# Row sums turned in two 64-row pieces, six score banks in rotation, and a clear and four scatters moved

## The chip, the cores and the metric

The kernel runs on one core of one Trainium2 chip. The metric is the device time of one execution in microseconds (us). Five engines work side by side, each through its own instructions in order, and wait for each other by semaphores: TensorE (PE, matrix products and transposes), VectorE (DVE), ScalarE (ACT), GpSimd (POOL) and SyncE (SP, which issues most of the transfers).

## The reference

Three layers, all in float32:

```python
scores = q @ k.T / 8 + bias          # 2 batches, 8 heads, 768 rows, head size 64
scores = where(keep, scores, -1e9)   # keep: the 8 first columns and the last 96 before the row
a = exp(scores - max); a = a / (a.sum(-1) + 1e-9)
x = (a @ v)                          # 1536 x 512
h = x @ w_in; x = (h * sigmoid(h)) @ w_out          # 512 -> 2048 -> 512
e = argmax(x @ w_gate)               # one of 8 experts for each row
out = p[e] * sigmoid(x @ w_output_gate)[e] * (relu(x @ w1[e]) @ w2[e])
```

## The kernel before

The rows are cut in tiles of 128; a batch has six. Because of the band a tile of queries meets its own 128 keys and those of the tile before (whose place the global columns share). The **first batch** (tiles n = 0 to 5) is worked before everything else, in 24 **slots**: slot s = 4n + hp is the head pair hp of tile n. `slot_b(s)` writes the work of one slot as a pipeline over several head pairs:

- PE turns the exponentials of slot s-3 (`emit_tr`, L214: eight transposes of 64 rows, two row halves into two banks) and makes the scores of slot s+1 (`emit_qk`, L174) into other columns of the same two banks;
- DVE adds the bias table and finds the row minimum (`emit_tb`, L184, twice); ACT takes the exponential (`emit_exp`, L195, twice) and sums the row; ACT (DVE in the first eight slots) copies the turned tiles out (`emit_cp`, L220 or L221);
- PE multiplies the turned tile of slot s-4 with v (`emit_px`, L231) into the tile `px`, which is transposed: rows of it are head columns.

Once in four slots a tile is finished. DVE adds up and inverts the row sums (`emit_rs`), POOL spreads them over 512 columns (tile `rx`, L1043), PE turns `rx` (`emit_rb`, L238: four transposes of 128 rows into one bank, at the end of slot 4n+7), DVE copies the bank (L243) and multiplies `px` with it (L248), and POOL splits the product in a high and a low part (`put_xt`, L283 and L285). For n = 4 the turn stands at the end of slot 22, for n = 5 in slot 26, among the first steps of the next layer.

On the side the weights of the second layer, which come as 64-bit numbers, are decoded on DVE: `dec_op` puts nine single steps (L309, L310, L311 for three pieces of weight) into nine of the slots. Their scratch tile `dct` lies in a PSUM bank. POOL splits the decoded weights (L332, L339).

PSUM has eight banks. The score tiles (`xy`) and the turned sums (`rb`) rotate over five (`a`, `s20` to `s23`, by the counter `acnt`), `s1` and `pv` hold `px`, and `s1b` holds the warm-up products and then `dct`.

Slots 24 to 26 run beside the first steps of the second layer. Its loop has 5 x 16 steps: `s1_mm` (L361), `s1_ev`, `s1_sp`, `s2_mm` (L382 to L384, two steps behind), with chunk c = 0 being the tile pairs u = 0 and 1, and c = 1 to 4 one pair each. Beside chunks 1 to 3 the attention of the second batch runs (`slot`): there ACT's exponential is split in a high and a low half, the low half by POOL (`emit_l`, L202, for three of four head pairs), and both are transposed by a DMA (L205) before PE uses them (`emit_pv`, L260). Finished pairs pass the gates, one small part in each step from a queue `gq`: `gate1` (turn), `gate2` (logits), `gate3` (ranks, factor, and the first scatter of 128 rows to the DRAM table `xe`), `gate4` (the second scatter, L523, by POOL's own DMA). `rows_clear(0)` writes empty rows into the first window of `xe` from a zero tile, and later calls copy that window to the others.

The order on each engine is the order in which these functions are called; no scheduler moves anything.

Of the kernel before, what the change touches and what calls it, by code (L numbers as in the profile page):

```python
# [10 lines left out]
F32 = mybir.dt.float32  # L11
# [8 lines left out]
P = 128  # L20
# [3 lines left out]
def kernel(ctx, tc, qk, v, n_global, n_local, w_in, w_out, wg, w1, w2, out):  # L24
# [6 lines left out]
    SB=24  # L31
# [48 lines left out]
    wm=[]  # L80
    def warm(k):

        if not wm: wm.append(ps.tile([P,512],F32,tag="s1b",name="wm",bufs=1))
        for _ in range(k): T.matmul(wm[0].rearrange("p (a b) -> p a b",a=4),ones,ones[:,None,:].to_broadcast([P,4,P]),start=True,stop=True)
    def spread():

# [42 lines left out]
            if h%2 if dst.start<3 else h<2: (G if dst.start<3 else V).tensor_scalar(out=tabs[:,dst,h,:],in0=tabm['w'][0][:,3,src],scalar1=-8.0*2.0**-(h+1),scalar2=None,op0=ALU.mult)  # L129
            else: A.activation(out=tabs[:,dst,h,:],in_=tabm['w'][0][:,3,src],func=AF.Copy,scale=-8.0*2.0**-(h+1))  # L130

    atags=[['a','s20','s21','s22','s23']]; acnt=[0]; ded=[False]
    def abank(shape,name):
        tg=atags[0][acnt[0]%len(atags[0])] if not ded[0] else 'a'; acnt[0]+=1
        return ps.tile(shape,F32,tag=tg,name=name,bufs=1)
# [97 lines left out]
    rb={}  # L233
    def emit_rb(n):

        r=rs.pop(n)
        m=abank([P,KC,P],"rb")
        for k in range(KC): T.transpose(m[:,k,:],r[:,k*P:(k+1)*P],ident)  # L238
        rb[n]=m
        if n==SB//4-1: rb_copy(n,A)  # L240
    def rb_copy(n,e):
        m=rb[n]; x=rb[n]=attn.tile([P,KC,P],F32,tag="t",name="xn",bufs=3)
        if e is V: V.tensor_copy(x,m)  # L243
        else: A.activation(out=x,in_=m,func=AF.Copy)
    def emit_xx(n):
        if n<SB//4-1: rb_copy(n,V)
        x=rb.pop(n)
# [54 lines left out]
    def dct(tag):  # L302

        if tag not in pst: pst[tag]=ps.tile([P,512],I32,tag=tag,name="dct",bufs=1)
        return pst[tag]
# [18 lines left out]
    def dec_op():  # L324
        if not dops: return
        k,st=dops.pop(0)
        if st==0: wF[k]=mp.tile([P,512],I32,tag="wt",name="wt",bufs=2)
        r=wraw[k]; decode(wF[k],r[:,:,0],r[:,:,1],(st,),dct('s1b'))
        if st==2: del wraw[k]; wst[1,k%2]=k//2+1
    def spl_w(k,first=False):  # L330
        def cast(o,i):
# [87 lines left out]
    def rows_clear(e):  # L419
        win=lambda e: XE[e*CAP:e*CAP+WROWS,:].rearrange("(a p) d -> p a d",p=P)  # L420
        S.dma_start(win(e),win(0) if e else zr[0][:,None,:].to_broadcast([P,WROWS//P,XW]))
# [586 lines left out]
    def own(n): return 4*(n+2)>=SB  # L1008
    def slot_b(s):

        ev=[]
        n5,h5=divmod(s-LT-2,4); o5=0<=s-LT-2<SB
        n,hp=divmod(s,4); n1,h1=divmod(s-1,4); n3,h3=divmod(s-LT,4); n4,h4=divmod(s-LT-1,4)
        n2,h2=divmod(s-2,4); cur=s<SB; o1=0<=s-1<SB; o2=0<=s-2<SB; o3=0<=s-LT<SB; o4=0<=s-LT-1<SB
        def a_():
            if s<SB-3: want(min(s+WL,SB-1))
            elif cur: want(s+3)
            if s==0:
                m=two()
                for j in range(2): emit_qk(n,hp,j,m)  # L1020
            if cur: emit_tb(n,hp,0)
            if s+1<SB or o3: m=two()
            if o3: cp[0]=emit_tr(n3,h3,m)
            if s+1<SB:
                for j in range(2): emit_qk(*divmod(s+1,4),j,m)
            if s<3: warm(2)
            if s>=SB and o3: emit_cp(*cp[0],V)
            if o1 and s<SB: emit_exp(n1,h1)
            for d,h in TB.get(s-1,()):
                if d==0: tab_heads(slice(0,2),slice(0,2),(h,))  # L1030
        ev.append(a_)
        def a2():
            if cur: emit_tb(n,hp,1)
            if o3 and s<SB: emit_cp(*cp[0],A if DQ<=s<23 else V)
            if o1 and s>=SB: emit_exp(n1,h1)
            if o4: emit_px(n4,h4)
            if o3 and h3==3 and own(n3): emit_rb(n3)
            if o4 and h4==3 and not own(n4): emit_rb(n4)
            if o5 and h5==3 and not own(n5): emit_xx(n5)
            if o2 and h2==3:  # L1040
                for k in range(2): emit_rs(n2,k)
                r=attn.tile([P,512],F32,tag="t",name="rx",bufs=3)
                G.tensor_copy(r.rearrange("p (h d) -> p h d",h=H),rs[n2].to_broadcast([P,H,D])); rs[n2]=r  # L1043
        ev.append(a2)
        def b_():
            if cur: glob_k(n,hp)
            if h4==3 and o4 and own(n4): emit_xx(n4)
            if s==0: table(slice(0,3),(0,1))
            if s==1: table(slice(0,3),(2,))
            for d,h in TB.get(s,()):  # L1050
                if d: tab_heads(slice(2,3),slice(2,3),(h,))
            if hp==3 and 4*(n+1)<SB and cur: load_v(n+1)
        ev.append(b_)
        return ev
# [42 lines left out]
    with tc.manual_schedule():  # L1097
        params()
        want(7); load_v(0)
        table_ints()  # L1100
        warm(4)
        table_floats(slice(3,4),V)
        spread()
        warm(1)
        table(slice(3,4))
        table_floats(slice(0,3),A)
        tab_heads(slice(3,4),slice(3,4),range(H))
        rows_init()
        s=0
        while s<SB:  # L1110
            for k,e in enumerate(slot_b(s)):
                e()
                if k==0 and s in DQS: dec_op()
            if s==6: rows_clear(0)
            s+=1
            for x in WP.get(s,()): w_to(*x)
        atags[0]=['s20','s21','s22','s23']
        steps=[(c,f) for c in range(len(CH)) for f in range(FB)]
        pend=[]
        gq=[]  # L1120
        def run_ev(k):
            for _ in range(min(k,len(pend))): pend.pop(0)()
        def run_gates(k):
            for _ in range(min(k,len(gq))): gq.pop(0)()
        for g in range(len(steps)+LAG):
            live=g<len(steps)
            if live:
                c,f=steps[g]
                if g==4*FB: ded[0]=False
                if c==0:  # L1130
                    w_to(0,0,g+LI); w_to(0,1,g+(LO if g<LS else 1)); w_to(2,0,f+1)
                for u in CH[c]: s1_mm(u,f)
                for u in CH[c]: s1_ev(u,f)
                if c==0:
                    for _ in range(2 if g==0 else 1):
                        if s<SB+4: pend+=slot_b(s); s+=1
                    if g==3: atags[0]=['a']; gate_consts()
                    if g==8: gate_parts()
                    if f==FB-1: s=SB
                elif c<4 and s<NS+4 and (f>1 and f!=8 if c==1 else f%2==0):  # L1140
                    pend+=slot(s); s+=1
                run_ev((1,2,1,1,1)[c])
                for u in CH[c]: s1_sp(u,f)
                dec_rest()
                run_ev(5 if c==0 else 2 if c==1 else 3 if f%2 else 0)
                if g<=FB:
                    w_to(1,0,g+2); w_to(2,1,g-1); w_to(1,1,g)
                if g in (1,2,10,11,12,13,14): rows_clear(g if g<3 else g-7)
                if g==FB: load_v(SB//4)
            if g>=LAG:  # L1150
                c2,f2=steps[g-LAG]
                s2_mm(c2,f2)
                if live and g>=LAG+FB: run_gates(2 if g-(len(CH)-1)*FB in (2,4) else 1)
                if f2==FB-1:
                    first_=[lambda u=u: s2_ev(u) for u in CH[c2]]
                    if c2==0: first_.append(lambda: (atags.__setitem__(0,['a','s22','s23']),ded.__setitem__(0,True)))
                    gq[:0]=first_
                    at=len(gq)
                    for u in CH[c2]:
                        seq=[lambda n=n,fn=turn if u in PU else gate1: fn(n) for n in (2*u,2*u+1)]  # L1160
                        if u in PU: seq=[lambda u=u,fn=fn: fn(u) for fn in (piece1,piece2,piece3,piece4)]+seq+[lambda: None]*2
                        seq.append(lambda u=u: gate2(u))
                        if u==1: seq.append(lambda: None)
                        seq+=[lambda u=u,fn=fn: fn(u) for fn in (gate3,lambda u: gate4(u,1))]
                        for i,fn in enumerate(seq):
                            if at+i<len(gq): gq[at+i]=lambda fs=(gq[at+i],fn): [f() for f in fs]
                            else: gq.append(fn)
                        at=len(gq)-(4 if u in PU else 0)
                    run_gates(3 if c2==0 else 1)
                    if c2==len(CH)-2: gq.append(lambda: order(0))  # L1170
                    if c2==len(CH)-2: gq.append(moe2_open)
            if live and c>0:
                if f==0: load_wol(c,0); load_wol(c,1)
                if f+2<FB: load_wol(c,f+2)
            if g>=len(steps)-FB: moe2_pre(g-len(steps)+FB)
        moe2()
# [68 lines left out]
```

## Time and profile before

| | us |
|---|---|
| median of 3 runs (lowest to highest) | 560.42 (560.03 to 561.67) |
| the profiled execution's own time | 559.99 |
| its span, first to last instruction | 558.3 |
| PE busy | 546.5 (98%) |
| DVE busy | 379.7 (68%) |
| ACT busy | 310.2 (56%) |
| POOL busy | 168.0 (30%) |

The page cuts the span in 40 slices of 14 us. In the first three DVE, ACT and POOL are much busier than later (DVE 7, 9, 9 tenths; ACT 7, 9, 8; POOL 5, 7, 7), while PE shows 9 from the first to the last but one. A view by stretches gives busy microseconds of each engine; "x" is the number of instructions. In a timeline a row has start, duration, engine, line, operation and tiles, and in brackets how long its engine stood idle before it and what ended that. Rows may be merged, so a duration beside "x8" is that of all eight; where PE's rows overlap, the distance of starts is the cost.

### The profile page before, as it was taken

What the parts mean: (1) busy time and instruction counts of PE and PEld (TensorE: products, weight loads), DVE (VectorE), ACT (ScalarE), POOL (GpSimd) and SP (SyncE); (2) the same over time, 40 slices, a digit from 0 to 9 for tenths busy, and PEclk for the clock granted to TensorE, in tenths of its full rate; (3) what the DMA queues carried; (4) which work ended last, traced back from release to release, by engine and by line L of the source; (5) the groups of instructions that cost most, each with busy time, mean ns of one, the idle gap of its engine ahead of it and who ended that gap; (6) DMA issues with size and microseconds to landing.
All of it is one profiled execution on the core that took longest, in us unless ns stands there. A gap on an engine that the chain in (4) does not pass through costs nothing.

```text
span 558.3 us, 12046 instructions
## 1 busy us (share of the span) xinstructions
PE 546.5 (98%) x4048; PEld 467.7 (84%) x4048; DVE 379.7 (68%) x1114; ACT 310.2 (56%) x824; POOL 168.0 (30%) x231
## 2 busy tenths in 40 slices
PE   9999999999999999999999999999999999999993
PEld 4668999998888888888998989889887888888882
DVE  7997988883678737474634457548775976977950
ACT  7984444443654645445523436627755776867740
POOL 5775978673242430323001010210011010010011
PEclk9999999999999999999999999999999999999997
DMA  6763987995594877765593359129773967868500
GB/s 188 249 226 135 317 285 223 290 300 176 157 206 127 199 183 155 175 148 122 132 174 114 93 164 368 59 89 322 254 238 116 288 197 234 258 208 276 160 21 23
DMA packets 87531, 106.76 MB, mean 191 GB/s; under 512 B 35980, under 2 KB 50316, under 8 KB 87460
## 3 DMA queue, kind: packets, MB, share of 16 engines
q1 hardware_dynamic: 84980, 99.25, 60.7%
q0 software_dynamic: 2192, 6.39, 3.1%
q8 instruction: 34, 0.56, 0.4%
q14 instruction: 37, 0.30, 0.2%
q10 hardware_dynamic: 288, 0.26, 0.2%
HBM read 87.14 MB, written 17.66 MB: 188 GB/s over the span
## 4 chain that ended last, share of the span: by engine, by line
PE 81%; POOL 7%; issue 5%; DMA 3%; DVE 1%; ACT 1%; SPq 1%; POOLq 0%; ACTq 0%
PE s L361 20%; PE h L721 7%; PE s L382 6%; PE s L384 6%; PE s L383 6%; PE h L722 4%; PE y L754 4%; PE y L755 4%; PE y L756 4%; PE xy L174 3%; PE h L727 2%; PE pv L260 2%; POOL wol L345 2%; POOL g L371 2%; PE y L750 2%
## 5 line engine op out<-in xcount | busy, mean ns | idle before, releaser
L361 PE MATMUL s<-xT,wi 128*128 128x256 f32 x1152 | 152.5, 284 | 0.0
L361 PEld LDWEIGHTS s<-xT,wi 128*128 128x128 f32 x1152 | 147.2, 191 | 5.4 <-issue 0.3
L365 ACT ACTIVATE u<-s 128x256 f32<-128x256 f32 x96 | 36.4, 380 | 98.8 <-PE s L361 94.4
L382 PE MATMUL s<-woh,g 128*128 128x512 f32 x192 | 78.4, 408 | 0.0
L592 DVE TENSOR_TENSOR uq<-qr,uq 128x512 fp32r<-128x512 f32 x112 | 74.5, 689 | 3.3 <-ACT uq L591 1.4
L383 PE MATMUL s<-woh,g 128*128 128x512 f32 x192 | 75.6, 394 | 0.0
L367 DVE SCALAR_TENSOR_TENSOR s<-u,s 128x256 f32<-128x256 f32 x64 | 27.3, 426 | 60.1 <-ACT u L365 60.1
L591 ACT ACTIVATE uq<-qr 128x512 fp32r<-128x512 f32 x112 | 66.6, 625 | 1.4 <-DMA qr<-in_w_dram 1.4
L678 POOL DMA_INDIRECT out_dram<-y,ixt x17 | 19.0, 1120 | 154.3 <-ACT y L767 94.5
L195 ACT ACTIVATE t<-t,mx 128x256 f32<-128x256 f32 (+1 forms) x96 | 46.0, 485 | 0.4 <-DVE mx L184 0.3
L202 POOL TENSOR_TENSOR hl<-t,hl 128x512 f16<-128x512 f32 (+1 forms) x18 | 19.6, 1087 | 85.8 <-ACT g L370 37.4
L382 PEld LDWEIGHTS s<-woh,g 128*128 128x128 f32 x192 | 36.3, 189 | 6.9 <-issue 1.8
L383 PEld LDWEIGHTS s<-woh,g 128*128 128x128 f32 x192 | 36.3, 189 | 5.1
L384 PE MATMUL s<-wolr,g 128*128 128x512 f32 x128 | 39.8, 392 | 0.0
L371 DVE TENSOR_TENSOR g<-s,g 128x256 fp32r<-128x256 f32 x64 | 27.0, 422 | 16.3 <-ACT g L370 13.8
L734 DVE TENSOR_TENSOR h<-h,hs 128x192 f32<-128x192 f32 (+5 forms) x56 | 20.9, 373 | 25.3 <-ACT hs L733 25.2
L754 PE MATMUL y<-uq,hh 128*128 128x512 f32 (+1 forms) x88 | 36.7, 417 | 0.0
L370 ACT ACTIVATE g<-s 128x256 fp32r<-128x256 f32 x64 | 24.2, 378 | 21.4 <-DVE s L367 21.3
L755 PE MATMUL y<-uq,hh 128*128 128x512 f32 (+1 forms) x88 | 34.6, 394 | 0.0
L756 PE MATMUL y<-uq,hh 128*128 128x512 f32 (+1 forms) x88 | 34.6, 393 | 0.0
L736 ACT ACTIVATE hh<-h 128x192 fp32r<-128x192 f32 (+5 forms) x56 | 19.7, 352 | 24.9 <-DVE h L734 15.5
L721 PE MATMUL h<-xwT,uq 128*128 128x448 f32 (+5 forms) x144 | 32.5, 347 | 0.0
(283 smaller groups left out, 1097.8 us busy)
## 6 DMA issues: line engine op xcount, KB each, us to landing
qr<-in_w_dram SPq DMA_DIRECT2D x128, 256.0 KB
wolr<-wlo_d SPq DMA_DIRECT2D x64, 256.0 KB
wiraw<-in_w_in_dram SPq DMA_DIRECT2D x16, 512.0 KB
wraw<-in_w_out_dram SPq DMA_DIRECT2D x13, 512.0 KB
ring<-in_qk_dram SPq DMA_DIRECT2D x22, 256.0 KB
xe<-xe SPq DMA_DIRECT2D x7, 792.0 KB
wlo_d<-wol SPq DMA_DIRECT2D x16, 256.0 KB
xw<-xe SPq DMA_DIRECT2D x15, 264.0 KB
```

Of the source, the lines that this page charges most:

```text
L195: A.activation(out=t[:,j,:ce],in_=t[:,j,:ce],func=AF.Exp,scale=-1.0 if 4*n<SB else 0.125,bias=mx[n][:,h:h+1],accum_out=ss[n][:,h,0:1])
L361: T.matmul(t,w[:,ww,kc,:],x[:,xx,kc,:],start=(k==0),stop=(k==11)); k+=1
L371: (G if u_ in CH[0] else V).tensor_tensor(out=g[:,1],in0=t,in1=g[:,0],op=ALU.subtract)
L382: T.matmul(o,g[u][:,0,sl],wh,start=(f==0),stop=False)
L383: T.matmul(o,g[u][:,1,sl],wh,start=False,stop=False)
L384: else: T.matmul(o,g[u][:,0,sl],wl,start=False,stop=(f==FB-1))
L591: A.activation(out=t[:,0],in_=r,func=AF.Copy)
L592: (G if (i%2 if pool is None else pool) else V).tensor_tensor(out=t[:,1],in0=r,in1=t[:,0],op=ALU.subtract)
L721: for kc in range(KC): T.matmul(t[:,:2*W],uq[4*p+2*(f//4),kc][:,0,s],xwT[p,kc][:,:,:W],start=(kc==0),stop=False)
L754: T.matmul(o,hi,w[:,0],start=(f==0),stop=False)
L755: T.matmul(o,g[:,z:z+n],w[:,0],start=False,stop=False)
L756: T.matmul(o,hi,w[:,1],start=False,stop=(f==7))
```

## The change

- `emit_rb` takes two banks of the rotation by `two()` and turns the spread sums in eight transposes of 64 rows, as `emit_tr` does. It stands in the first part of a slot, behind `emit_tr` and ahead of the scores: for n = 0 to 4 in slot 4n+7 (n = 4 goes from slot 22 to 23), for n = 5 in slot 26. `rb_copy` copies two halves instead of one tile.
- `s1b` joins the rotation, which has six banks now, and the counter starts from 0 again after `spread`. The warm-up goes to `s1`. The nine decode steps lose their bank: they work in their result tile `wt`, in SBUF.
- `rows_clear(0)` is issued in slot 16 instead of slot 6.
- For the pairs u = 0 to 3 the second scatter stands one step later in the gate queue; so what follows it in the queue (the gates of u = 1 behind those of u = 0) also moves by a step.

```diff
-        if not wm: wm.append(ps.tile([P,512],F32,tag="s1b",name="wm",bufs=1))
+        if not wm: wm.append(ps.tile([P,512],F32,tag="s1",name="wm",bufs=1))
...
-    atags=[['a','s20','s21','s22','s23']]; acnt=[0]; ded=[False]
+    atags=[['s1b','a','s20','s21','s22','s23']]; acnt=[0]; ded=[False]
...
-        r=rs.pop(n)
-        m=abank([P,KC,P],"rb")
-        for k in range(KC): T.transpose(m[:,k,:],r[:,k*P:(k+1)*P],ident)
-        rb[n]=m
-        if n==SB//4-1: rb_copy(n,A)
+        x=rs.pop(n); m=rb[n]=two()
+        for k in range(KC):
+            for r in range(2):
+                o=slice(r*D,(r+1)*D)
+                T.transpose(m[r][:,k*D:(k+1)*D],x[o,k*P:(k+1)*P],ident[o,o])
     def rb_copy(n,e):
         m=rb[n]; x=rb[n]=attn.tile([P,KC,P],F32,tag="t",name="xn",bufs=3)
-        if e is V: V.tensor_copy(x,m)
-        else: A.activation(out=x,in_=m,func=AF.Copy)
+        for r in range(2):
+            o=x[:,:,r*D:(r+1)*D]; i=m[r][:,:KC*D].rearrange("p (k q) -> p k q",k=KC)
+            if e is V: V.tensor_copy(o,i)
+            else: A.activation(out=o,in_=i,func=AF.Copy)
...
-        r=wraw[k]; decode(wF[k],r[:,:,0],r[:,:,1],(st,),dct('s1b'))
+        r=wraw[k]; decode(wF[k],r[:,:,0],r[:,:,1],(st,))
...
             if o3: cp[0]=emit_tr(n3,h3,m)
+            if o4 and h4==3 and n4<SB//4-1: emit_rb(n4)
+            if o3 and h3==3 and n3==SB//4-1: emit_rb(n3)
             if s+1<SB:
                 for j in range(2): emit_qk(*divmod(s+1,4),j,m)
...
-            if o3 and h3==3 and own(n3): emit_rb(n3)
-            if o4 and h4==3 and not own(n4): emit_rb(n4)
+            if o3 and h3==3 and n3==SB//4-1: rb_copy(n3,A)
...
         spread()
+        acnt[0]=0
...
-            if s==6: rows_clear(0)
+            if s==16: rows_clear(0)
...
-                        seq+=[lambda u=u,fn=fn: fn(u) for fn in (gate3,lambda u: gate4(u,1))]
+                        seq+=[lambda u=u: gate3(u)]+[lambda: None]*(u<4)+[lambda u=u: gate4(u,1)]
```

PE, slots 10 to 13 of the kernel before (`xy` are the score banks, `t` exponentials, `ring` queries and keys, `rx` the spread sums of tile 1, `px` the products with v):

```order
L214 MATMUL xy<-ident,t 128x64 x8
L174 MATMUL xy<-ring_77 128x256 x2
L231 MATMUL px<-pT_383,vpr 64x128 x4
L214 MATMUL xy<-ident,t 128x64 x8
L174 MATMUL xy<-ring_76 128x256 x2
L231 MATMUL px<-pT_417,vpr 64x128 x4
L238 MATMUL rb<-ident,rx 128x128 x4
L214 MATMUL xy<-ident,t 128x64 x8
L174 MATMUL xy<-ring_76 128x256 x2
```

The same place of the changed kernel:

```order
L214 MATMUL xy<-ident,t 128x64 x8
L174 MATMUL xy<-ring_77 128x256 x2
L231 MATMUL px<-pT_388,vpr 64x128 x4
L214 MATMUL xy<-ident,t 128x64 x8
L240 MATMUL xy<-ident,rx 128x64 x8
L174 MATMUL xy<-ring_76 128x256 x2
L231 MATMUL px<-pT_421,vpr 64x128 x4
L214 MATMUL xy<-ident,t 128x64 x8
L174 MATMUL xy<-ring_76 128x256 x2
```

The turn of the sums moved ahead of the scores and the product of its slot, and four transposes became eight smaller ones.

POOL, the gates of pair u = 1 in the kernel before (`xr` gated rows, `gdi` their places, `hl` split exponentials, `vraw` and `vpr` values; the DMA rows are scatters):

```order
L517 COPY xr<-tok 128x2
L523 DMA xe<-xr,gdi 12288x528
L202 TENSOR_TENSOR hl<-t,hl 128x2x256
L154 TENSOR_TENSOR vpr<-vraw,vpr 128x512
L523 DMA xe<-xr,gdi 12288x528
L202 TENSOR_TENSOR hl<-t,hl 128x2x256 x2
L150 TENSOR_TENSOR vraw<-vraw,vpr 128x512
```

The same gates in the changed kernel:

```order
L202 TENSOR_TENSOR hl<-t,hl 128x2x256
L154 TENSOR_TENSOR vpr<-vraw,vpr 128x512
L519 COPY xr<-tok 128x2
L525 DMA xe<-xr,gdi 12288x528
L202 TENSOR_TENSOR hl<-t,hl 128x2x256
L525 DMA xe<-xr,gdi 12288x528
L202 TENSOR_TENSOR hl<-t,hl 128x2x256
L150 TENSOR_TENSOR vraw<-vraw,vpr 128x512
```

Both scatters moved behind the split of the values, and one split of exponentials stands on each side of the second.

SP, the transfers of slots 5 to 8 before (`ring` queries and keys, `xe<-zr` the clear, `wiraw` weights):

```order
L141 DMA ring_77<-in_qk_dram 128x2x256
L141 DMA ring_76<-in_qk_dram 128x2x256
L421 DMA xe<-zr 128x3x528
L144 DMA vpr<-in_v_dram 128x512
L295 DMA wiraw<-in_w_in_dram 128x4x256
L141 DMA ring_77<-in_qk_dram 128x2x256
```

Where the clear stands in the changed kernel:

```order
L144 DMA vpr<-in_v_dram 128x512
L141 DMA ring_77<-in_qk_dram 128x2x256
L423 DMA xe<-zr 128x3x528
L301 DMA woraw<-in_w_out_dram 128x1024
L144 DMA vpr<-in_v_dram 128x512
L297 DMA wiraw<-in_w_in_dram 128x4x256
```

The clear moved behind the last load of queries and keys for the first batch.

## Rows read from the trace of the kernel before

**Rows 1.** Stretch, its length, busy PE, PEld, DVE, ACT, POOL, clock, DMA share, GB/s:

```profile
14.50:25.60 11.10, 10.92 (x142) 7.25 (x140) 10.96 (x45) 10.42 (x42) 8.91 (x18) 1.00 0.90 282
25.60:41.00 15.40, 15.40 (x201) 10.20 (x197) 13.37 (x55) 14.42 (x57) 11.29 (x22) 1.00 0.64 212
...
60.00:140.00 80.00, 80.00 (x506) 72.64 (x506) 61.60 (x105) 35.90 (x84) 56.74 (x83) 1.00 0.80 262
```

**Rows 2.** Chain that ended last, slots 14 and 15: start, us, what:

```profile
26.84 0.49 PE xy L174 x4
27.33 0.59 PE px L231 x8
27.92 0.59 PE rb L238 x4
28.50 0.39 PE xy L214 x8
```

**Rows 3.** Timeline of slots 10 and 11, around the turn of tile 1:

```profile
19.42 0.61 POOL L1043 COPY rx<-rs 128x512 f32<-128x512 f32 x1
...
19.53 0.46 PE L214 MATMUL xy<-ident,t 64*128 64x64 f32 x8
...
19.71 0.42 DVE L184 CUSTOM_DVE_ANT_1 t<-xy,tabs 128x256 f32<-128x256 f32 x1
...
20.99 0.66 PE L238 MATMUL rb<-ident,rx 128*128 128x128 f32 x4
```

**Rows 4.** DVE by line and shape, first 46 us: count, then busy us, mean ns:

```profile
L243 DVE COPY xn<-rb 128x512 f32<-128x512 f32 x5 | 3.4, 684 | 0.0
L220 DVE COPY pT<-xy 128x256 f32<-128x256 f32 x7 | 2.6, 416 | 0.3 <-PE xy L214 0.3
...
L124 DVE TENSOR_SCALAR wk<-wk,pf 128x384 f32<-128x384 f32 x1 | 0.4, 414 | 0.0
...
L124 DVE TENSOR_SCALAR wk<-wk,pf 128x128 f32<-128x128 f32 x1 | 0.3, 287 | 0.0
```

**Rows 5.** Timeline, two places where DVE and POOL both work in SBUF:

```profile
179.86 1.16 POOL L150 TENSOR_TENSOR vraw<-vraw,vpr 128x512 f32<-128x512 f32 x1
...
180.02 1.02 DVE L506 CAST gdi<-gsm 128x2 uint32<-128x2 f32 x1
...
358.56 1.28 POOL L625 TENSOR_TENSOR ehl<-xr,ehl 128x512 fp32r<-128x512 f32 x1 [5.60 <-ACT ehl L624]
...
359.03 1.36 DVE L625 TENSOR_TENSOR ehl<-xr,ehl 128x512 fp32r<-128x512 f32 x1 [2.32 <-ACT ehl L624]
```

**Rows 6.** Timeline, two decode steps and the POOL operations beside them:

```profile
18.06 1.27 POOL L285 TENSOR_TENSOR xT<-xn,xT 128x512 fp32r<-128x512 f32 x1
...
19.11 0.69 DVE L310 SCALAR_TENSOR_TENSOR dct<-wiraw,dct 128x512 int32<-128x512 int32 x1
...
36.63 0.61 POOL L283 CAST xT<-xn 128x512 fp32r<-128x512 f32 x1 [0.49 <-DVE xn L248]
...
36.81 0.68 DVE L311 SCALAR_TENSOR_TENSOR wt<-wiraw,dct 128x512 int32<-128x512 int32 x1
```

**Rows 7.** Timeline, the clear's issue and the one load that PE waits for:

```profile
14.32 0.60 SPq L421 DMA_DIRECT2D xe<-zr  x1
...
23.69 0.30 PEld L174 LDWEIGHTS xy<-ring 64*128 64x128 f32 x4 [0.32 <-DMA ring<-in_qk_dram]
```

**Rows 8.** Timeline around the second scatter of pair u = 1:

```profile
187.86 0.99 POOL L523 DMA_INDIRECT xe<-xr,gdi  x1 [1.64 <-DMA xe<-xr,gdi]
188.87 1.18 POOL L202 TENSOR_TENSOR hl<-t,hl 128x512 f16<-128x512 f32 x1
...
195.01 0.76 PE L260 MATMUL pv<-vpr,pT 128*128 128x64 bf16 x20 [0.81 <-DMA pT<-hl]
```

**Rows 9.** Chain that ended last, the transfer between those two:

```profile
190.07 4.88 DMA pT<-hl
```

**Rows 10.** DVE's line L592 over the whole span: ns min/median/max, first and last start:

```profile
L592 DVE TENSOR_TENSOR uq<-qr,uq x112: 672/685/968, 339.5 to 529.5; 128x512 fp32r<-128x512 f32 x112
```

## The prediction

> **What bounds the kernel now.** I read the page's shares first: PE is busy for 98% of the span, so a gain must shorten PE's own work or one of its few waits. Then the view by stretches. From 60 to 140 us PE is busy for 80.00 of 80.00 us [rows 1]: a microsecond won before that point arrives at the end unless a transfer falls behind. Then the chain of waits in the first batch, because most of the change lies there. It runs from one PE group to the next, with nothing between: a slot is 0.49 (scores) + 0.59 (product with v) + 0.39 (turned exponentials) = 1.47 us, and a slot with a turn of sums has 0.59 more [rows 2]. By that chain PE alone bounds slots 12 to 23.
>
> The stretches warn against reading this alone. From 14.5 to 25.6 us DVE is busy for 10.96 of 11.10 us, more than PE's 10.92, with ACT at 10.42; from 25.6 to 41 PE has 15.40 of 15.40, ACT 14.42, DVE 13.37, POOL 11.29 [rows 1]. So up to slot 13 DVE is as much the bound as PE, and behind it a shorter PE has some 1.0 us (15.40 - 14.42) until ACT is the bound. Last I looked for PE's waits: 0.32 us at 23.69 for a load [rows 7] and 0.81 us at 195.01 for a transposing transfer [rows 8].
>
> **The change part by part.**
>
> *The turns.* Four transposes of 128 rows take 0.59 us; the eight of 64 rows have the shape of the turned exponentials, which take 0.39 [rows 2]. Six turns save 6 x 0.20 = 1.2 us of PE, five of them before 41 us and one in the full stretch behind. All of it is on PE's path, except where PE now waits in front of the turn. The turn moves up by a score group and a product, 0.49 + 0.59 = 1.08 us. What it needs has not moved: the spread sums from POOL, and its two banks. In slot 11 PE could begin it at 19.53 + 0.39 = 19.92. The spread sums end at 19.42 + 0.61 = 20.03, and one of the banks was last read by DVE's second score pass of slot 10, which ends at 19.71 + 0.42 = 20.13 [rows 3]. So PE waits 0.21 us there; before, the turn stood at 20.99 and waited for neither. Behind the waiting turn stand the scores of slot 12, for which ACT's copy and then DVE wait. I take 0.2 for slot 11 and another 0.2 for the turns of tiles 0, 2, 3 and 4 together: +0.4 (0 to +1.0, five such waits).
>
> *The copies.* One DVE copy of 512 columns, 0.684 us, becomes two of 256. Their rows show 0.416, but DVE starts the next before the last has ended, and 0.684 against 2 x 0.416 = 0.83 bounds the difference: 0 to +0.15 each [rows 4]. I take 0.
>
> *The decode steps.* Nine DVE instructions read and write SBUF only, where a PSUM bank served before. Alone they should cost the same: a two-input DVE instruction in SBUF with 512 columns has a median of 0.685 us [rows 10], the decode step 0.69 [rows 6]. But beside POOL it is different. At 359.03 the same kind of instruction took 1.36 us: POOL's own had begun at 358.56 and ended at 359.84, and DVE's was over 0.55 us behind that. A cast of two columns took 1.02 us from 180.02, until POOL's operation ended at 181.02 [rows 5]; the longest of the 112 two-input rows is 0.968 [rows 10]. So these six two-input steps will wait when POOL is in the middle of an operation. Laid on the trace of before: the step at 19.11 would wait until 18.06 + 1.27 = 19.33, 0.22 us, and the one at 36.81 until 36.63 + 0.61 = 37.24, 0.43 us [rows 6]. The other four start where POOL is between operations or about to start, and then POOL waits. I take +0.65, the sum of the two; from below 0, from above all nine steps at the mean of the two, 9 x 0.33 = +3.0. The first lies where DVE has 0.14 us of slack in 11.10 [rows 1]; the second has more room, but I count both in full.
>
> The Trainium skill says the same as a rule, and it speaks against this part of the change: in "SBUF — State Buffer", section "Who interferes with whom", a DVE instruction with two SBUF inputs and a POOL instruction that reads SBUF exclude each other, and the later one waits for the whole of the other. The rows at 359.03 agree (1.36 instead of 0.69 us). The other three steps have one input. "VectorE: DVE Perf Modes" of the Trainium skill, section "Mode 2×_2P", lets such an instruction run at twice the rate from SBUF to SBUF, holding the shared port meanwhile; L124 at 0.414 for 384 columns and 0.287 for 128 agrees for float32 [rows 4], and no run here shows it for this integer form with every second word read. By it the sum would have 3 x 0.2 us less on DVE, and three more waits.
>
> *The clear.* The clear's transfer goes out of slots 6 to 12 into those from slot 16 on, behind the last load of queries and keys that the first batch needs. The load that made PE wait 0.32 us at 23.69 [rows 7] comes earlier. DVE is full there, so I count 0; the gain is at most 0.32. The weights queued behind the clear in its new place are wanted only in the second layer, and the DMA share falls from 0.90 to 0.64 in that stretch [rows 1]: 0.
>
> *The scatters.* For pair u = 1 POOL stood 1.64 us before the second scatter, until the first had landed. The split of exponentials behind it began at 188.87, its transfer ran 4.88 us from 190.07, and PE waited 0.81 us [rows 8, 9]. Now the first scatter stands in front of that split and the second behind. The split can begin some 1.6 us earlier, of which the first scatter's 0.99 may take up to 0.99 back: between 0.65 and 1.64 earlier against a wait of 0.81. I take the whole wait as gone, -0.81 (0 from above). The gates of u = 1 move by one or two steps as a whole; PE has no other wait there to lengthen, and POOL is idle for most of those steps.
>
> *The sum*, against the profiled execution's 559.99: -1.2 + 0.4 + 0 + 0.65 + 0 - 0.81 = -0.96, so 559.03. That execution was 0.43 below the median of the runs, 560.42; as a median, 559.5. Its own range takes the ends of each term: all gains and no cost, -1.2 - 0.32 - 0.81 = -2.3 (558.1); the dearer DVE waits at half their bound and a scatter that gains nothing, -1.2 + 0.4 + 1.5 = +0.7 (561.1).
>
> **The rivals.**
>
> *DVE and POOL don't collide*, because in the new order the steps fall between POOL's operations. For it: POOL is idle for 2.2 of 11.1 us and 4.1 of 15.4 [rows 1]; against it the two pairs in rows 6. Then the DVE term is 0 and the load's wait counts: -1.2 + 0.4 - 0.32 - 0.81 = -1.93, 558.5.
>
> *The turns wait for POOL* (slower). A decode step holds POOL back for up to 0.69 us, and between two turns POOL has to do L283, L285 and the spreading in a row. Two such blocks move the end of the spread sums in slot 11 from 20.03 to 21.41, and PE stands from 19.92 until then, with the next scores behind it: 1.49 us. For the three turns with decode steps around them that is 4.5 us, less the 1.2 and 0.81: +2.5, 562.9. For it: the turn has lost its 1.08 us of lead, and POOL is busy for 80% of the first stretch. Against it: most steps start beside no POOL operation. It decides from 0.67 us for each of the three turns (2.0 / 3); below that the kernel is not slower.
>
> *The scatters' place changes nothing*: the 4.88 us of the transfer are themselves a queue behind other transfers, and PE waits as before. For it: the DMA engines are busy there. Against it: the transfer starts right behind the split. Then 560.3.
>
> **How the numbers follow.** Chances: my forecast 0.55 at 559.5, no collisions 0.20 at 558.5, turns waiting for POOL 0.12 at 562.9, scatters for nothing 0.13 at 560.3. A measurement of this kernel can tell about 0.3%, 1.7 us, from no change: faster means below 558.7, slower above 562.1. Faster: the 0.20, and a ninth of the forecast's share whose costs stay out, 0.06, together 0.26. Slower: 0.12. Within: 0.62. The range from 558.0 to 561.6 leaves out the slower rival for the most part and a little below.
>
> **What would show it.** In the changed trace: L240 at about 0.39 us for eight; the wait of PE before it and its releaser (DVE's L184 or POOL's `rx`); the decode rows L311 to L313 longer than 0.69 us where a POOL row ends within them; no wait for a load near 23.69; the first product of the second layer (L361 before) between 0.5 us earlier and 0.5 later than now; PE's wait at L260 near 195 gone. I am wrong if the decode rows stay at 0.69 while the stage still gains nothing, if PE stands for more than 0.67 us before the turns, or if a new wait appears in chunk 1.

## The result, and the profile after

| | before | after |
|---|---|---|
| median (lowest to highest), us | 560.38 (560.03 to 561.67), 6 runs | 566.01 (565.11 to 566.74), 6 runs |
| span of the profiled execution, us | 558.3 | 563.7 |
| PE busy, us | 546.5 | 546.3 |
| POOL busy, us | 168.0 | 170.9 |

The ratio is 1.0100, 95% interval 1.0087 to 1.0112: slower by 5.6 us, where 559.5 was forecast and 561.6 was the range's upper end. PE does no more work; it waits more. The view of waits sums PE's idle time by what ended it (total, times, longest):

```profile
PE xy L240 <- POOL rx L1046: 2.8, 3, 1.1
PE gl L473 <- DVE xT L287: 2.2, 1, 2.2
...
PE h L723 <- ACT eyo L677: 0.8, 1, 0.8
PE px L231 <- POOL vpr L163: 0.4, 1, 0.4
```

None of these four stood in the kernel before; its one large wait, for `pT` at 195.01 [rows 8], is gone. To see where the lateness arises I took the same matmul in both traces:

| place (start before, us) | later in the changed kernel by |
|---|---|
| scores ahead of the first turn (12.15) | -0.23 |
| product of slot 10, behind the first turn (18.94) | -0.39 |
| first product of slot 11 (20.40) | +1.15 |
| first batch over, L361 (41.96) | +1.89 |
| chunk 1 under way (154.37) | +1.50 |
| behind the logits of u = 1 (183.00) | +5.27 |
| behind the place of the old wait (199.88) | +4.48 |
| first h of the last stage (375.44) | +5.47 |
| near the end (530.53) | +5.35 |

The first -0.23 is the start of the program (between -0.2 and +1.0 in the profiled executions, also of kernels that are not changed there), the next -0.16 the first turn, for which PE did not wait. So there are three losses and one gain: first batch +2.1, gates +3.8, the last stage +1.0, and -0.8 for the old wait. The -0.4 ahead of chunk 1 is a wait for a load of weights (at 142.38 in the kernel before) that comes and goes between executions of all these kernels.

**The first batch.** The stretches answer [rows 1] (PE, PEld, DVE, ACT, POOL busy, clock, DMA share, GB/s); the second is longer here, since the batch ends later, and the last one is the place behind the logits:

```profile
14.50:25.60 11.10, 10.03 (x142) 6.71 (x144) 10.37 (x42) 10.01 (x40) 8.57 (x16) 1.00 0.61 184
25.60:42.80 17.20, 15.05 (x212) 9.77 (x210) 15.17 (x60) 14.88 (x58) 13.69 (x22) 1.00 0.72 247
60.00:140.00 80.00, 80.00 (x509) 72.78 (x508) 63.27 (x107) 34.85 (x80) 58.59 (x85) 1.00 0.83 268
178.20:181.70 3.50, 3.50 (x29) 3.28 (x26) 1.53 (x9) 0.21 (x1) 0.00 (x0) 0.51 0.58 137
```

Before, PE was idle for 0.18 us in the first and not at all in the second; now it is idle for 1.07 and 2.15 us, though no other engine is full either: they wait for each other in turn. The timeline answers [rows 3] and shows how:

```profile
19.14 0.46 PE L214 MATMUL xy<-ident,t 64*128 64x64 f32 x8
...
19.20 0.80 DVE L312 SCALAR_TENSOR_TENSOR wt<-wiraw,wt 128x512 int32<-128x512 int32 x1
...
19.40 0.67 POOL L159 COPY ring<-ring 128x32 f32<-128x32 f32 x1
...
20.01 0.61 POOL L1046 COPY rx<-rs 128x512 f32<-128x512 f32 x1
...
20.67 0.46 PE L240 MATMUL xy<-ident,rx 64*128 64x64 f32 x8 [1.07 <-POOL rx L1046]
...
20.97 0.65 PE L174 MATMUL xy<-ring 64*128 64x256 f32 x4
...
24.63 0.42 DVE L311 TENSOR_SCALAR wt<-wiraw 128x512 int32<-128x512 int32 x1
...
24.68 0.84 POOL L285 CAST xT<-xn 128x512 fp32r<-128x512 f32 x1
...
32.83 1.28 POOL L287 TENSOR_TENSOR xT<-xn,xT 128x512 fp32r<-128x512 f32 x1
...
33.15 1.23 DVE L311 TENSOR_SCALAR wt<-wiraw 128x512 int32<-128x512 int32 x1
...
34.04 0.41 POOL L159 COPY ring<-ring 128x32 f32<-128x32 f32 x1
...
34.39 0.61 POOL L1046 COPY rx<-rs 128x512 f32<-128x512 f32 x1
...
35.05 0.46 PE L240 MATMUL xy<-ident,rx 64*128 64x64 f32 x8 [1.09 <-POOL rx L1046]
```

POOL's copy of 32 columns (0.21 us otherwise) took 0.67 beside the decode step and ended just after it. `rx`, next on POOL, came 0.59 later than before, and PE stood from 19.60 to 20.67 with the scores of slot 12 behind the turn. At 33.15 the decode step was the late one (1.23), behind POOL's split of 32.83, and POOL's copy then waited for it in turn. The groups of the first 46 us (count, busy us, mean ns) show the collisions as a whole:

```profile
L312 DVE SCALAR_TENSOR_TENSOR wt<-wiraw,wt 128x512 int32<-128x512 int32 x3 | 2.6, 861 | 0.0
L311 DVE TENSOR_SCALAR wt<-wiraw 128x512 int32<-128x512 int32 x3 | 2.4, 786 | 0.0
L313 DVE SCALAR_TENSOR_TENSOR wt<-wiraw,wt 128x512 int32<-128x512 int32 x3 | 2.4, 786 | 0.0
...
L159 POOL COPY ring<-ring 128x32 f32<-128x32 f32 x16 | 4.8, 305 | 0.0
```

The decode steps cost 7.4 us instead of 6.2 (9 x 0.69 [rows 6]), and POOL's sixteen small copies alone 4.8 instead of 3.2.

**The gates of u = 1.** Timeline of PE and DVE:

```profile
173.54 0.63 PE L279 MATMUL ms<-ident,xa 128*128 128x128 f32 x4
...
174.94 0.62 PE L386 MATMUL s<-wolr,g 128*128 128x512 f32 x2
...
176.03 0.69 DVE L202 TENSOR_TENSOR hl<-t,hl 128x512 f16<-128x512 f32 x1
...
177.06 0.68 DVE L287 TENSOR_TENSOR xT<-ms,xT 128x512 fp32r<-128x512 f32 x1
177.80 0.86 PE L473 MATMUL gl<-wgb,gx 128*128 128x48 bf16 x24 [2.23 <-DVE xT L287]
...
178.49 2.91 PE L363 MATMUL s<-xT,wi 128*128 128x256 f32 x12
```

In chunk 1 one bank, `a`, serves the gates' tiles and the turned attention rows `ms` (`abank` while `ded` is set). Before, the logits `gl` took it first, then `ms`:

```profile
170.03 0.77 PE L471 MATMUL gl<-wgb,gx 128*128 128x48 bf16 x24
...
170.64 1.67 PE L361 MATMUL s<-xT,wi 128*128 128x256 f32 x12
...
172.75 0.64 PE L277 MATMUL ms<-ident,xa 128*128 128x128 f32 x4
```

The empty step of u = 0 moved the gates of u = 1 one step on, so `ms` takes the bank first, and `gl` waits until DVE, with its queue of that slot, has read it: 2.23 us. Behind this wait the granted clock fell to 0.51 over the stretch 178.2 to 181.7 (1.2 GHz); twelve L363 took 2.91 us, where twelve took 1.67 before.

**The last stage:**

```profile
375.60 4.49 PE L674 MATMUL ey<-uq,eg 128*128 128x512 f32 x18
...
380.17 0.69 ACT L677 ACTIVATE eyo<-ey,ex 128x512 f32<-128x512 f32 x1 [3.69 <-PE ey L674]
...
380.91 0.96 PE L723 MATMUL h<-xw,qb 128*128 128x384 f32 x4 [0.82 <-ACT eyo L677]
```

Here the rotation is `s1`, `s1b`, `a`, `pv`, and `ey` lies in `pv`. The counter stands at 99 where it stood at 94: the first `h` gets bank 99 mod 4 = 3, `pv`, instead of 2, `a`, and must wait until ACT has read `ey`. Before, it followed `ey` without a wait:

```profile
371.12 4.48 PE L672 MATMUL ey<-uq,eg 128*128 128x512 f32 x18
375.44 0.86 PE L721 MATMUL h<-xw,qb 128*128 128x384 f32 x4
```

### The profile page after: what moved, and what is told of

Its sections match the earlier page's. It is cut to its first block, busy times and chain, and to the rows that moved or that the text cites. A ratio compares the mean times of both kernels' runs of the same rounds, so it can differ in the third digit from the quotient of the medians.

```text
span 563.7 us, 12103 instructions
## 1 busy us (share of the span) xinstructions
PE 546.3 (97%) x4072; PEld 468.3 (83%) x4072; DVE 380.7 (68%) x1119; ACT 310.8 (55%) x825; POOL 170.9 (30%) x231
## 4 chain that ended last, share of the span: by engine, by line
PE 91%; POOL 3%; DVE 2%; issue 1%; DMA 1%; ACT 1%; SPq 0%; POOLq 0%; ACTq 0%; DVEq 0%
PE s L363 24%; PE s L384 8%; PE s L385 8%; PE s L386 8%; PE h L723 7%; PE h L724 4%; PE y L756 4%; PE y L758 4%; PE y L757 4%; PE xy L174 3%; PE pv L262 2%; PE h L729 2%; PE y L752 2%; PE y L751 2%; PE xm L713 1%; PE px L231 1%
## 5 line engine op out<-in xcount | busy, mean ns | idle before, releaser
L363 PE MATMUL s<-xT,wi 128*128 128x256 f32 x1152 | 153.7, 286 | 0.1
L363 PEld LDWEIGHTS s<-xT,wi 128*128 128x128 f32 x1152 | 148.4, 192 | 5.6 <-DVE xn L250 0.3
```

The costliest lines, as they stand in the source:

```text
L363: T.matmul(t,w[:,ww,kc,:],x[:,xx,kc,:],start=(k==0),stop=(k==11)); k+=1
```

## The experiments

Theory: three separate losses, the early turns together with the collisions, the gates' step, and the bank counter. Rivals: the late first batch makes the later waits; or the collisions alone are the loss.

**gates_before**, the changed kernel with

```diff
-seq+=[lambda u=u: gate3(u)]+[lambda: None]*(u<4)+[lambda u=u: gate4(u,1)]
+seq+=[lambda u=u,fn=fn: fn(u) for fn in (gate3,lambda u: gate4(u,1))]
```

> The changed kernel with the gate queue of before: no empty step ahead of the second scatters. Theory (the loss has three separate places: turns in the first batch +1.9, the gates of u = 1 +3.9, the first h +0.9): the logits of u = 1 (L473) stand again one step ahead of the turn ms, take bank a before it, and the wait of 2.23 us and the slow clock behind it (about 1.6 us) go, while the wait for pT near 195 comes back with 0.87: 566.0 - 3.9 + 0.9 = 563.0. Rival (the late first batch shifts the whole of chunk 1 and makes that wait; the gates' order has no part in it): the wait at L473 stays and the one for pT comes on top: 566.0 to 566.9.

562.68 (ratio to before 1.0033, 1.0021 to 1.0045). The wait at the logits and the slow clock are gone. But the wait for `pT` did not come back, which neither theory had.

**gates_u1**, the changed kernel with

```diff
-[lambda: None]*(u<4)
+[lambda: None]*(0<u<4)
```

> The changed kernel with the empty step for u = 1 to 3 only, not for u = 0: the gates of u = 1 stand where they stood before, and only the second scatter is a step later. Theory (the empty step of u = 0 pushes the logits of u = 1 behind ms; the spacing of u = 1's own scatters is what removes the wait for pT): the wait at L473 and the slow clock go, -3.9, and the wait near 195 does not come back: 566.0 - 3.9 = 562.1. Rival (the wait for pT went because the whole group moved): as gates_before, 562.7 to 563.0.

562.10 (1.0036, 1.0022 to 1.0050), as the theory said: the step of u = 0 costs 3.9 us by the medians, 3.6 by the ratios. PE's waits here are those of the first batch and the last stage alone.

**gates_alone**, the kernel before with the change's line for the gates.

> The kernel before with one edit: the empty step ahead of the second scatter for u = 0 to 3. Theory (the empty step of u = 0 alone puts the logits of u = 1 behind ms on bank a; nothing of the first batch is needed for it): PE waits about 2.2 us at the logits (L473 in the changed kernel), the wait near 195 goes: 560.4 + 2.2 + 0.6 - 0.9 = 562.3, and 563.7 if the clock falls as in the changed kernel. Rival (the late first batch made the wait): 560.4 - 0.9 = 559.5.

562.65 (1.0044, 1.0028 to 1.0060). The first batch is as before, and the same wait stands at the logits:

```profile
177.22 1.05 PE L471 MATMUL gl<-wgb,gx 128*128 128x48 bf16 x24 [2.23 <-DVE xT L285]
178.09 2.86 PE L361 MATMUL s<-xT,wi 128*128 128x256 f32 x12
```

So the late first batch has no part in it; that rival falls. That the bank makes the wait is read from the program, where `gl` reads nothing of `ms` or `xT`; no run gives `gl` a bank of its own. The clock fell in this execution too, but not in each: the six runs gave 563.27 to 564.30 where the mean granted clock was 0.991 or 0.992, and 561.34 to 562.03 where it was 0.995. By these two groups the fall costs about 1.8 us; by the traces, 1.5 (the gates cost 3.8 us with it and 2.3 in turns_behind_px without). The changed kernel's runs do not show it: five of six have 0.991 or 0.992, and the one with 0.996 took 565.96, no less than the others.

**h_bank**, the changed kernel with

```diff
-        atags[0]=['s1','s1b','a','pv']
+        atags[0]=['s1','s1b','a','pv']; acnt[0]+=3
```

> The changed kernel with three added to the bank counter where the last stage begins, so that its first h takes the bank it had before and not the one of ey. Theory (ACT's reading of ey holds the bank): PE's wait of 0.82 before the first h (L723) goes, 566.0 - 0.87 = 565.1, all else as it is. Rival (a transfer that lands late holds h, and the releaser named is only the last one seen): the wait stays, 566.0.

564.97 (1.0083, 1.0063 to 1.0103), 1.0 less than the changed kernel. `h` follows `ey` at once (before this it waited 0.82):

```profile
378.76 1.55 PE L674 MATMUL ey<-uq,eg 128*128 128x512 f32 x6
380.14 0.86 PE L723 MATMUL h<-xw,qb 128*128 128x384 f32 x4
```

**turns_behind_px**, the changed kernel with the two calls of `emit_rb` moved from the front of the slot to behind `emit_px`.

```diff
-            if o4 and h4==3 and n4<SB//4-1: emit_rb(n4)
-            if o3 and h3==3 and n3==SB//4-1: emit_rb(n3)
...
+            if o3 and h3==3 and own(n3): emit_rb(n3)
+            if o4 and h4==3 and not own(n4): emit_rb(n4)
```

> The changed kernel with the turns at their old place behind px (for n = 4 in slot 22), still 64 rows and two banks, decode steps still in SBUF. Theory (the waits come from the turn having lost 1.08 us of lead): PE's waits before L240 fall from 2.8 us in all to 0.5 or less, the first batch ends at most 0.4 later than before instead of 1.9: 566.0 - 1.6 = 564.4. Rival (POOL and DVE, which hold each other up, are late whatever the place): PE waits as long, for rx or for the copies of exponentials: 565.5 to 566.0.

563.66 (1.0059, 1.0041 to 1.0077), 2.35 less, more than the theory's 1.6. Its trace gives 1.6 for the first batch; the rest can be the clock, since one run in six had a mean granted clock below 0.994, where five of the changed kernel's had. No wait stands before L240. Left are the waits at the logits and at `h`, and two groups for POOL, behind operations of it that a decode step lengthened:

```profile
PE gl L473 <- DVE xT L287: 2.2, 1, 2.2
...
PE xy L174 <- POOL ring L159: 0.9, 2, 0.5
PE px L231 <- POOL vpr L163: 0.9, 1, 0.9
```

In this execution the wait of 2.23 us at the logits was not followed by a slower clock:

```profile
177.90 1.68 PE L363 MATMUL s<-xT,wi 128*128 128x256 f32 x12
```

**decode_sbuf**, the kernel before with

```diff
-decode(wF[k],r[:,:,0],r[:,:,1],(st,),dct('s1b'))
+decode(wF[k],r[:,:,0],r[:,:,1],(st,))
```

> The kernel before with one edit: the nine decode steps work in their result tile in SBUF and not in a PSUM bank. Theory (collisions lengthen DVE and POOL by 1 to 3 us, but the turns at the end of their slots cover it): decode steps with a mean of about 0.8 us instead of 0.69, the first batch later by 0 to 0.6: 560.4 to 561.0. Rival (the collisions alone make the first batch late): 560.4 + 1.9 = 562.3.

561.58 (1.0019, 1.0007 to 1.0031): +1.1, between the two. The late one is `vpr`, behind POOL's split of weights, not a turn:

```profile
34.04 1.07 POOL L332 CAST wi<-wt 128x512 fp32r<-128x512 f32 x1
...
36.56 0.61 POOL L163 COPY vpr<-vpr 32x512 f32<-32x512 f32 x1
...
37.22 0.44 PE L231 MATMUL px<-pT,vpr 128*64 128x128 f32 x4 [0.65 <-POOL vpr L163]
```

**decode_px_bank**, the changed kernel with the decode scratch in the bank of `px` that is idle for four slots:

```diff
-    DQS=(9,10,11,13,15,17,18,19,21)
+    DQS=(9,10,11,13,14,15,17,18,19)
...
+        if st==0: pst['d']=ps.tile([P,512],I32,tag=('s1','pv','s1')[k//2],name="dct",bufs=1)
-        r=wraw[k]; decode(wF[k],r[:,:,0],r[:,:,1],(st,))
+        r=wraw[k]; decode(wF[k],r[:,:,0],r[:,:,1],(st,),pst['d'])
```

> The changed kernel with the decode scratch back in PSUM, in the bank of px that is idle for four slots (s1, pv, s1 for the three pieces), and the steps in slots 9, 10, 11, 13, 14, 15, 17, 18, 19 so that each piece fits there; turns still ahead of the scores. Theory (the collisions of DVE and POOL in SBUF make rx and vpr late): decode steps 0.69 us, POOL's L159 back to 0.21 us, PE's waits before L240 under 0.3 us each, the first batch ends 1.9 + 0.5 earlier than in the changed kernel: 566.0 - 2.4 = 563.6. Rival (the lead of 1.08 us that the turn lost is what counts): L240 still waits about 0.7 us three times, 565.5.

563.21 (1.0060, 1.0044 to 1.0077), 2.8 less, of which the trace gives 1.6 to the first batch; the clock fell in fewer of these runs too (two of six below 0.994). The collisions are gone, and more than half of the wait is left:

```profile
L312 DVE SCALAR_TENSOR_TENSOR dct<-wiraw,dct 128x512 int32<-128x512 int32 x3 | 2.1, 691 | 0.0
...
L159 POOL COPY ring<-ring 128x32 f32<-128x32 f32 x16 | 3.2, 209 | 0.0
```

```profile
PE xy L240 <- POOL rx L1046: 1.6, 3, 0.6
```

Both theories hold in part. What the first batch costs, as lateness at 41.96 less lateness at 12.15, ahead of the first turn:

| | turns behind px | turns ahead of the scores |
|---|---|---|
| decode in PSUM | -0.5 (all_mended_behind) | +0.6 (decode_px_bank) |
| decode in SBUF | +0.5 (turns_behind_px) | +2.1 (changed kernel) |

Either costs 1.0 to 1.1; together they cost 2.7, more than the sum: the early turn has no slack left to take POOL's delay (its waits are 1.6 us without the collisions and 2.8 with them). The kernels of the upper row also have five decode steps in earlier slots; decode_sbuf, where the slots stay as before, puts the collisions alone at 1.0 as well.

**all_mended** (decode_px_bank, gates_u1 and h_bank together) and **all_mended_behind** (the same with the turns behind px):

> decode_px_bank, gates_u1 and h_bank together: the turns in 64 rows ahead of the scores, with none of the three losses. Theory (the losses are separate and add): 566.0 - 2.4 - 3.9 - 0.9 = 558.8. Rival (they overlap, or the early turns still wait): 560 to 561.

> all_mended with the turns behind px, at their old place. If the early place costs nothing once POOL is on time: as all_mended, 558.8. If the early place costs its waits: 0.5 to 1.0 below all_mended.

559.83 (0.9997, 0.9987 to 1.0006) and 559.16 (0.9973, 0.9965 to 0.9982). The losses add up, but to 1.0 less than forecast: 2.4 us had been taken for the collisions, and the trace gives them 1.6. The early place costs 0.7 by the medians and 1.3 by the ratios (expected 0.5 to 1.0), and the second kernel beats the kernel before by 0.3%, and the changed one. (Its profiled execution, 560.23, is the longest of its eleven: PE waits 1.0 there for the bank of `xm`, behind a late load of weights.)

**turns_128**, all_mended_behind with

```diff
-        x=rs.pop(n); m=rb[n]=two()
...
+        x=rs.pop(n); m=rb[n]=abank([P,KC,P],"rb")
+        for k in range(KC): T.transpose(m[:,k,:],x[:,k*P:(k+1)*P],ident)
```

one copy instead of two, and the counter set so that the later stages take the banks they had before.

> all_mended_behind with the turns in four transposes of 128 rows into one bank, and one copy. Theory (PE bounds the first batch, so the eight transposes of 64 rows, 0.30 us a turn instead of 0.59, are worth nearly 6 x 0.29 = 1.7 us): 559.2 + 1.5 = 560.7. Rival (DVE and POOL bound as much, so a PE that is done sooner only waits): 559.2 to 559.5.

559.41 (0.9985, 0.9976 to 0.9993): 0.25 more by the medians and 0.7 by the ratios, whose intervals overlap, not 1.5. The first batch ends nearly at the same time: by the table's measure -0.1 at 41.96 and -0.3 at 109.46 with turns of 128 rows, -0.5 at both with those of 64. With 64 rows PE waits 0.49 us there for `vpr` and 0.18 for DVE; with 128 it has neither of these waits, but 0.26 at L358 behind them. So of PE's 1.7 us 0.2 to 0.5 arrive by the traces.

**scatter_u1** (the kernel before with the line of gates_u1) and **clear_6** (all_mended_behind with `if s==6: rows_clear(0)`):

> The kernel before with one edit: the empty step ahead of the second scatter for u = 1 to 3 only. Theory (spacing the scatters of u = 1 takes PE's wait for pT away and moves nothing else): 560.4 - 0.9 = 559.5, no wait of PE between 60 us and the last stage. Rival (the gain needs the later chunk 1 of the changed kernel): 560.4.

> all_mended_behind with the clear issued in slot 6 again. Theory (the clear delays the load of queries and keys by PE's 0.2 to 0.3 us near 23.7 and nothing else): 559.2 + 0.3 = 559.5. Rival (in slot 16 it delays something of equal size): 559.2 or less.

559.72 (0.9994, 0.9986 to 1.0003) and 559.82 (0.9989, 0.9978 to 0.9999). Both are less clear than the theories. In clear_6 the wait for `pT` is back, though the scatters stand apart. Its rows, then those of all_mended_behind:

```profile
188.20 1.25 SPq L205 DMA_TRANSPOSE pT<-hl  x1
...
194.78 0.76 PE L262 MATMUL pv<-vpr,pT 128*128 128x64 bf16 x20 [0.78 <-DMA pT<-hl]
```

```profile
188.38 1.26 SPq L205 DMA_TRANSPOSE pT<-hl  x1
...
194.10 0.76 PE L262 MATMUL pv<-vpr,pT 128*128 128x64 bf16 x20
```

The transfer was issued 0.18 earlier and landed later, 6.53 us after its issue by the chain of waits. That transfer's length varies, whatever stands ahead of it. What the move does give it is time: it is issued 5.7 us before PE needs it here, and 4.1 before that in the kernel before (190.07 against 195.01 - 0.81).

**scatter_off** (all_mended_behind with the gates' line of before), **clear_16** (the kernel before with `if s==16: rows_clear(0)`) and **two_moves** (clear_16 and scatter_u1 together, nothing of the turns):

> all_mended_behind with the second scatters at their old place. Theory A (the spaced scatters of u = 1 take PE's wait for pT away): the wait of 0.8 near 195 is back, 559.2 + 0.8 = 560.0. Theory B (the wait comes and goes with how long the transfer of pT takes, whatever the scatters): no change beyond 0.3: 559.2 to 559.5.

> The kernel before with one edit: the clear in slot 16 and not in slot 6. Theory (it takes PE's wait of 0.2 to 0.4 for a load near 23.7 away): 560.4 - 0.3 = 560.1. Rival (it frees a transfer that the traces so far don't show, and is what the best kernel owes its lead to): 559.5 or less.

> The kernel before with the two moves alone: the clear in slot 16, and the second scatter a step later for u = 1 to 3. Turns, banks and decode as before. Theory (the turns of 64 rows gain nothing, since the first batch ends where it did with turns of 128): as all_mended_behind, 559.2. Rival (the smaller turns are worth their 1.7 us of PE in part): 559.8 or more.

559.68 (0.9983, 0.9970 to 0.9996), 559.87 (0.9988, 0.9978 to 0.9998), 559.12 (0.9972, 0.9962 to 0.9983). In scatter_off the wait for `pT` was absent, so theory A does not hold for each execution. Of the profiled executions with the scatters at their old place three show it (kernel before, decode_sbuf, clear_16) and two don't (gates_before, scatter_off); of twelve with the move one does (clear_6), and seven of these twelve are free of the wait at the logits. The move makes the wait rarer; by the ratios it is worth 0.3 to 0.9 us, each with an interval of about half a us to either side. The clear alone is worth 0.7 by its ratio (0.1 to 1.2), and 0.9 and 1.2 by the two other pairs that differ in it alone (all_mended_behind and clear_6, two_moves and scatter_u1). Its trace ends the first batch 0.3 earlier, without the wait of rows 7; but scatter_u1, with the clear in slot 6, has no such wait either and ends it as early. So no trace shows where the clear's gain lies. two_moves is as fast as all_mended_behind without anything that concerns the turns or the sixth bank; no run changes the sixth bank by itself.

## Why the prediction was wrong

- *Turns, -1.2.* The size on PE was too small: eight transposes take 0.30 us (20.67 to 20.97), so a turn is cheaper by 0.29, not 0.20. But at most 0.5 us of the 1.7 arrives (turns_128), and two_moves is as fast without it. The prediction had read that DVE is as much the bound as PE up to slot 13 and ACT 1.0 us behind it later [rows 1], and yet counted PE's whole saving: this term failed.
- *Waits before the turns, +0.4.* Measured 2.8 in three waits. Without collisions they are 0.56, 0.41 and 0.59 (decode_px_bank), where 0.2 was taken for slot 11 and 0.2 for four others together. Slot 11 was read from rows; the others were a guess, and the rows of slot 11 were taken as they stood. In decode_px_bank PE came to that turn at 19.74, 0.25 before the 19.99 of the kernel before, and `rx` ended at 20.25, 0.22 later.
- *Copies, 0.* No run tells them apart: a pair took 0.75 us for 0.684 [rows 4].
- *Decode steps, +0.65.* Alone they cost 1.1 (decode_sbuf), within the bounds of 0 to 3. But they were costed as DVE's time, and the price was paid by POOL's queue: its small copies, the casts and `rx` or `vpr` behind them. The Trainium skill, "SBUF — State Buffer", section "Who interferes with whom", says that the order of issue decides who blocks, and that the first has the shared port for its whole instruction; the rows at 19.20 and 19.40 agree for POOL as the one blocked. The case of one input, which no run had shown, is here as well: a decode step that began just before POOL's cast took 0.42 us at 24.63 instead of 0.69, and the cast 0.84 instead of 0.61; behind a POOL operation, at 33.15, the step took 1.23. "VectorE: DVE Perf Modes" of the Trainium skill, section "Mode 2×_2P", lets such an instruction make two results per cycle from SBUF to SBUF; 0.42 us against 0.69 agrees in kind.
- *Clear, 0.* Worth 0.7 by clear_16, whose interval reaches down to 0.1; the prediction allowed 0.32 at most. The wait for a load near 23.69 is gone, as foreseen, but it is also gone where the clear stands in slot 6 (scatter_u1, clear_6): that it came out so shows nothing of the clear.
- *Scatters, -0.81.* The step that failed worst: "The gates of u = 1 move by one or two steps as a whole; PE has no other wait there to lengthen". PE had none, but the move changed the order of two tiles on one bank, which cost 2.23 us and in most runs some 1.5 more by the clock. The mechanism of the gain itself was right (the transfer has 1.6 us more), but it was taken in full from one execution, while the wait comes and goes.
- *Not in the sum at all:* the bank counter. It was read that the counter starts from 0 again, but not where it would stand at the end: about 1.0 us in the last stage.
- *The rivals.* "Turns wait for POOL" was the right mechanism for the first batch: it put 1.49 us on each of three turns and called the kernel slower from 0.67 on, and they waited 1.07, 0.63 and 1.09. The gates and the counter, 4.8 us, stood in no rival.
- *The range.* It is said to take the ends of each term, but its upper end has the waits at 0.4 and not at 1.0, and the decode steps at half their bound. With both in full it is -1.2 + 1.0 + 3.0 = +2.8, 563.2 as a median; that, too, leaves out what was measured.
- *The signs of being wrong* were well chosen: two of the three came, more than 0.67 us before the turns and a new wait in chunk 1.

## What to carry to other kernels

Where tiles share a PSUM bank or rotate over banks by a counter, moving one step is a change of the order in which tiles take a bank, at each later place of that rotation; list those orders before and after, and look for a reader that is queued late. A saving on the engine that is busy all the time is worth something only where the others have slack: read the stretch, not the span. A wait seen in one profiled execution that hangs on a transfer's length should be priced by several executions.

## What the runs showed of the hardware that was not expected

- After PE had stood for 2.23 us the granted clock was 0.5 (1.2 GHz) in the changed kernel (178.3 to 181.7), h_bank and gates_alone, and stayed at 1.00 after the same wait in turns_behind_px and decode_px_bank. In gates_alone the runs with the lower mean clock are 1.8 us longer; the changed kernel's do not part in this way.
- A POOL copy of 32 columns, 0.21 us alone, took 0.67 beside a decode step of DVE in SBUF: a short instruction took three times its own length, and what was queued behind it on POOL came later with it (`rx` by 0.59). A decode step of one input that began just ahead of POOL's cast took 0.42 us (0.69 with its output in PSUM), and the cast 0.84 for 0.61.
